# The first expert layer of blocks 6 to 17 as a one-level Strassen step

## The chip, the cores and the metric

The kernel runs on one core of one Trainium2 chip. The core has a matrix engine (TensorE: PE for matmuls, PEld for loading their stationary operand), a vector engine (VectorE, DVE), a scalar engine (ScalarE, ACT), a general engine (GpSimd, POOL) and 16 DMA engines, whose transfers are all issued here from SyncE (SP). Each engine takes its instructions strictly in order, and waits at the head of its queue on semaphores of the others. Matmuls write to PSUM, of which the kernel uses 8 banks of 512 f32 words in each of 128 partitions; everything else lives in SBUF. The metric is the device time of one execution in microseconds (us).

## The reference

Attention over keys and values that are first averaged in groups of eight, then a two-layer expert with a rational function between the layers:

```python
k_p = k.reshape(B, H, Sp, pool, D).mean(axis=3)        # 8 x 8 heads, 576 -> 72 keys
v_p = v.reshape(B, H, Sp, pool, D).mean(axis=3)
attn = softmax(q @ k_p.T / sqrt(D))                    # with 1e-9 added to the sum
x = (attn @ v_p), heads side by side                   # 4608 tokens x 512
h = x @ w_in                                           # 512 -> 2048
P = a[0] + a[1] * h + a[2] * h*h + a[3] * h*h*h
Q = 1.0 + abs(b[0]) * abs(h) + abs(b[1]) * h*h
out = (P / (Q + 1e-06)) @ w_out                        # 2048 -> 512
```

## The kernel before

The 4608 tokens are 18 blocks of 256 (index i), the 2048 columns of d_ff are 8 units of 256 (index u). For each (i, u):

- `mm1` (L783) makes h in a PSUM tile `ph`, two groups of 128 columns by 256 tokens. Every f32 factor is split into a high and a low part, and three products are added (high x high, low x high, high x low). The width of 512 is four slices of 128, so this is 2 x 3 x 4 = 24 matmuls with 256 columns.
- `rational` and `quotient` (L796, L812) compute P / Q on 512 words per partition: six ACT operations, five of DVE and two of POOL, with the tiles `t`, `w`, `r` in SBUF and the bank `rp` in PSUM. They end with `gh` and `gl`, the high and low part of the result.
- `mm2` (L833) multiplies these by `wout` into two banks `po`, which collect over the 8 units: 12 matmuls with 512 columns.

Attention for a block (`attend`, L733) runs ahead of its eight units: scores `ps`, exponentials `e`, transposes (by DMA pieces into `am` from block 4 on, from `e` in 32 x 32 squares), values `pv`; `values` splits the block's x into two tiles by an ACT copy and a DVE subtraction. `load_weights` (L456) rebuilds each of the 16 weight tiles (`win0` to `win7`, `wout0` to `wout7`) from its loaded words, and they stay in SBUF. Blocks 0 and 1 go through units 0 to 3 first, their x is stored to HBM, and units 4 to 7 follow later with x loaded back (`xr`): the reloaded halves.

Nothing is issued as it is written. `Plan` collects the operations with their tile dependences, due times (`due`, L889) and costs, `solve` (L166) is a list scheduler on those numbers, and `issue` (L252) writes the resulting order out for each engine. Where that order leaves PE a gap, `issue` puts matmuls whose moving operand is zero: into the tile `idle` in the start, later into an open `po` bank, one after the other until the planned gap is full. They are called fillers here. The planner's numbers set the order alone; how long anything takes on the chip is up to the chip. PSUM's 8 banks are handed out by the same planner, and so are the numbered buffers of each pool.

Every instruction passes through one line of `issue`, L284 (fillers: L276), so the profile's rows are told apart by the names of tiles.

## Time and profile before

| | before |
|---|---|
| median of 3 runs | 944.45 us (944.35 to 945.45) |
| profiled execution, from first to last instruction | 943.9 us |
| granted TensorE clock | 1.000 |
| instructions of DVE, ACT, POOL | 1336, 1124, 463 |
| DMA: bytes moved, mean rate | 75.33 MB, 80 GB/s |

The page gives each engine's busy time as a share of the span, groups of equal instructions with their count, total and mean, and ahead of each group how long its engine was idle and what ended that. PE's end times are modelled, since matmuls are pipelined; start to start is the safer reading. Idle time of an engine that nobody waits for costs nothing. A transfer is given by its packets and by the time from issue to landing.

### The profile page before, as it was taken

The numbers are of one execution on the slowest core, as the hardware profiler recorded it, in microseconds if no ns is written. First come the engines' busy times: TensorE is split into PE (matmuls) and PEld (weight loads), VectorE is DVE, ScalarE is ACT, GpSimd is POOL, SyncE is SP. The second block draws the span as 40 slices with busy tenths as digits, with TensorE's granted clock in tenths as the row PEclk, the third lists the DMA queues.
The fourth block names the chain that finished last, engine by engine and source line by source line (L and its number), as shares of the span: only waits on it lengthen the run. The fifth ranks groups of instructions, "written<-read, shape, count | busy, mean of one in ns | idle before, by whom it ended". The sixth has DMA issues, their size and how long they took to land.

```text
span 943.9 us, 17079 instructions
## 1 busy us (share of the span) xinstructions
PE 932.3 (99%) x6152; PEld 845.0 (90%) x6152; DVE 786.0 (83%) x1336; ACT 693.7 (73%) x1124; POOL 528.0 (56%) x463
## 2 busy tenths in 40 slices
PE   8899999999999999999999999999999999999998
PEld 8888998989988899998999899998999899999996
DVE  7799988788989888887887997888898987887664
ACT  4788889868675877686776777676868595868674
POOL 4776866866446544445634574447545663544443
PEclk9999999999999999999999999999999999999999
DMA  9994201254235322122603160316222421202000
GB/s 275 313 390 160 45 29 46 67 127 87 49 81 105 86 34 47 29 56 53 138 5 75 51 140 8 54 37 139 47 36 50 97 50 28 51 1 57 1 23 23
DMA packets 185365, 75.33 MB, mean 80 GB/s; under 512 B 162624, under 2 KB 162624, under 8 KB 185280
## 3 DMA queue, kind: packets, MB, share of 16 engines
q1 hardware_dynamic: 185280, 74.23, 31.2%
q8 instruction: 49, 0.80, 0.4%
q14 instruction: 36, 0.29, 0.1%
HBM read 50.60 MB, written 12.58 MB: 67 GB/s over the span
## 4 chain that ended last, share of the span: by engine, by line
PE 87%; DMA 3%; SPq 3%; DVE 3%; POOL 1%; ACT 1%; issue 1%; POOLq 0%; ACTq 0%
PE ph L284 39%; PE po L284 39%; PE pv L284 4%; PE ps L284 4%; SPq L284 3%; DMA q<-in_q_dram 1%; DMA early<-in_v_dram 1%; DVE sm L284 1%; DMA st_v<-in_v_dram 1%; DVE t L284 1%; POOL w L284 0%; PE pvs L284 0%; ACT rp L284 0%; PE pq L284 0%; DVE mx L284 0%
## 5 line engine op out<-in xcount | busy, mean ns | idle before, releaser
L284 PEld LDWEIGHTS ph<-x,win 128*128 128x128 f32 x3264 | 472.7, 188 | 55.5 <-ACT w L284 0.8
L284 PE MATMUL ph<-x,win 128*128 128x256 f32 x3264 | 495.7, 282 | 1.4 <-DVE x L284 0.5
L284 PE MATMUL po<-wout,gh 128*128 128x512 f32 x1152 | 353.1, 397 | 0.1
L284 POOL TENSOR_TENSOR w<-w,r 128x512 f32<-128x512 f32 (+1 forms) x145 | 191.1, 1318 | 230.3 <-ACT r L284 228.1
L284 POOL TENSOR_TENSOR gl<-t,gh 128x512 fp32r<-128x512 f32 (+1 forms) x145 | 193.3, 1333 | 93.1 <-ACT gh L284 91.9
L284 PEld LDWEIGHTS po<-wout,gh 128*128 128x128 f32 x1152 | 185.7, 189 | 12.5 <-POOL wout L284 0.8
L284 PE MATMUL po<-wout,gl 128*128 128x512 f32 x576 | 181.8, 396 | 0.3 <-POOL gl L284 0.3
L284 ACT ACTIVATE rp<-w,cbias 128x512 f32<-128x512 f32 (+1 forms) x145 | 99.6, 687 | 59.8 <-POOL w L284 56.6
L284 DVE SCALAR_TENSOR_TENSOR t<-t,abn,rp 128x512 f32<-128x512 f32 (+1 forms) x145 | 107.3, 740 | 38.4 <-ACT rp L284 35.3
L284 DVE TENSOR_TENSOR t<-t,ph 128x512 f32<-128x512 f32 (+1 forms) x145 | 97.8, 675 | 48.7 <-ACT t L284 46.7
L284 ACT ACTIVATE r<-w,abn 128x512 f32<-128x512 f32 (+1 forms) x145 | 117.9, 813 | 20.8 <-POOL gl L284 11.4
L284 ACT ACTIVATE t<-ph,abn 128x512 f32<-128x512 f32 (+1 forms) x145 | 111.0, 767 | 26.3 <-PE ph L284 23.0
L284 ACT ACTIVATE w<-ph 128x512 f32<-128x512 f32 (+1 forms) x145 | 85.7, 591 | 40.8 <-PE ph L284 34.4
L284 DVE SCALAR_TENSOR_TENSOR t<-t,abn,ph 128x512 f32<-128x512 f32 (+1 forms) x145 | 107.0, 738 | 5.2 <-ACT w L284 1.3
L284 ACT CAST gh<-t 128x512 fp32r<-128x512 f32 (+1 forms) x145 | 88.3, 609 | 20.5 <-DVE t L284 16.9
L284 DVE SCALAR_TENSOR_TENSOR t<-rp,t 128x512 f32<-128x512 f32 (+1 forms) x145 | 99.4, 685 | 4.1
L284 DVE SCALAR_TENSOR_TENSOR rp<-w,rp 128x512 f32<-128x512 f32 (+1 forms) x145 | 99.0, 683 | 0.2
L284 PEld LDWEIGHTS po<-wout,gl 128*128 128x128 f32 x576 | 93.0, 189 | 6.4 <-POOL gl L284 0.5
L284 ACT ACTIVATE rp<-rp 128x512 f32<-128x512 f32 (+1 forms) x145 | 84.1, 580 | 3.6 <-DVE t L284 0.5
L284 POOL TENSOR_TENSOR e<-e,sm 128x576 f32<-128x576 f32 x36 | 41.8, 1175 | 51.2 <-DVE sm L284 38.7
L284 POOL TENSOR_TENSOR st_v<-st_v 128x512 f32<-128x512 f32 (+1 forms) x36 | 36.3, 1015 | 17.4 <-DMA st_v<-in_v_dram 10.7
L284 PE MATMUL ps<-kpT,qT 128*128 128x144 f32 (+1 forms) x320 | 45.6, 292 | 0.4 <-DVE kpT L284 0.2
(101 smaller groups left out, 855.9 us busy)
## 6 DMA issues: line engine op xcount, KB each, us to landing
am<-e SPq DMA_DIRECT2D x224, 48.0 KB, 2.1
out_dram<-ob SPq DMA_DIRECT2D x17, 512.0 KB, 3.1
rwin<-in_moe_w_in_dram SPq DMA_DIRECT2D x8, 1024.0 KB, 11.1
rwout<-in_moe_w_out_dram SPq DMA_DIRECT2D x8, 1024.0 KB, 14.1
st_k<-in_k_dram SPq DMA_DIRECT2D x12, 512.0 KB, 4.8
st_v<-in_v_dram SPq DMA_DIRECT2D x12, 512.0 KB, 4.2
q<-in_q_dram SPq DMA_DIRECT2D x144, 32.0 KB, 2.0
st_v<-in_v_dram SPq DMA_DIRECT2D x48, 64.0 KB, 2.2
```

The costliest lines, as they stand in the source:

```text
L284: getattr(engines[op.eng], name)(*map(value, args), **{k: value(v) for k, v in kw.items()})
```

## The change

For blocks 6 to 17, two neighbouring blocks go through the units together (a pair; with a unit, a pair-unit). Their h is a product of two 2 x 2 block matrices: two groups of 128 columns of d_ff by two halves of the width, times two halves of the width by two blocks. Instead of eight block products a one-level Strassen step (Winograd's form) makes seven, each of 2 slices x 3 split products = 6 matmuls with 256 columns. In order of issue they are called product 1 to 7 below:

- `combine` makes the seven combinations of x for a pair, four subtractions on POOL and seven splits into high and low part (ACT copy, POOL subtraction), once for the pair. `values` now only copies x out of PSUM.
- `combine_w` makes the seven combinations of each `win` tile once, in the stretch of blocks 4 and 5 and the reloaded halves, and stores them to HBM (`wd`). `fetch` loads them again for every pair-unit, in two loads of 1 MB and 0.75 MB into three buffers in turn; the room of `win0` to `win7` serves for this, for the combinations of x and for a second `e`.
- `mm1_both` runs the seven products in two banks, one of which is both blocks' `ph` tile by halves. Product 1 goes to the first half of bank A and product 2 to the second. ACT then copies the first half of A to the first half of B, and the second half of A to `ys` in SBUF. Product 3 adds into B, product 4 into the first half of A. DVE then writes B plus `ys` over the second half of A, product 5 adds to that, product 6 adds into B, DVE writes B plus `ys` into B's second half, and product 7 adds to B's first half.
- From block 6 on the quotient works in `ph` itself, with no bank for `rp`. The `po` banks of both blocks of a pair, four, are open at once.
- Blocks 4 and 5 go ahead of the reloaded halves. The planner's costs are other numbers, its random shifts of due times are gone, and two pools differ in size. Behind the transposes of k, two matmuls by zero now follow (`pk`, `pl`).

```diff
-    LAT = 0.07
-
-    BEGIN = {"sp": 0.8, "pe": 1.7, "pool": 1.3, "dve": 1.5, "act": 1.5}
+
+
+    TAIL = {"sp": 0.0, "pe": 0.16, "pool": 0.06, "dve": 0.09, "act": 0.1}
+    HOP = {"sp": 0.035, "pe": 0.035, "pool": 0.08, "dve": 0.035, "act": 0.035}
+
+    BEGIN = {"sp": 0.8, "pe": 2.1, "pool": 1.3, "dve": 1.5, "act": 1.5}
     WARM = 8.6
 
     LOOK = 0.02
 
-
-    MOVED, SHARE, REACH = 1850, 0.03, 4.0
-    SHIFTS = (600170, 650652, 293686, 721265, 222299, 972752, 932340, 238443, 467684, 409349, 642869, 707107)
+    RATE = 410e3
...
-                    self.nc.tensor.matmul(to, lhsT=self.filler, rhs=one, start=first, stop=first)
+                    self.nc.tensor.matmul(to, lhsT=self.filler, rhs=one, start=first, stop=first,
+                                          skip_group_check=True)
...
+    pool("ys", 1)
+    PLAIN, AHEAD, TURNS = 6, 7, 4
+    SOON, CWD = {4: 25, 5: 20, 6: 40, 7: 0}, 40
...
+    dve = Engine(plan, "dve", 0.068, 1.04)
+    act = Engine(plan, "act", 0.06, 0.85)
+    gp = Engine(plan, "pool", 0.14, 2.15)
...
+        if n > 1:
+            for x in (pk, pl):
+                pe(118, [mm(x[:, 0:TOK], identr, zero.to_broadcast([P, TOK]), True, True)])
...
+            if two:
+                act(2 * TOK).copy(whole[:, 2 * c + i % 2], pv.rearrange("p j t -> p (j t)"))
+                continue
...
+    OVER = lambda i, u: i >= PLAIN
...
+    def combine(k):
+
+        x = raw_x[k]
+        t = new("dec", "m", [P, 2, 2 * TOK], F32, f"tt{k}")
+        x11, x12, x21, x22 = (x[:, n] for n in range(4))
+        t3, t2 = t[:, 0], t[:, 1]
+
+        def minus(out, a, b):
+            gp(2 * TOK).tensor_tensor(out=out, in0=a, in1=b, op=ALU.subtract)
+
+        def put(n, src):
+            pair, half = divmod(n, 2)
+            if not half:
+                at = len(PAIRS) % 5
+                PAIRS.append(new("cpool", ("win0", "win1", "win2", "x0", "x1")[at],
+                                 [P, 2, 2, 2, TOK], F32R, f"x{k}_{pair}"))
+            to = PAIRS[-1]
+            src = src.rearrange("p (c t) -> p c t", c=2)
+            act(2 * TOK).copy(to[:, half, 0], src)
+            gp(2 * TOK).tensor_tensor(out=to[:, half, 1], in0=src,
+                                      in1=to[:, half, 0].bitcast(F32), op=ALU.subtract)
+            return to[:, half]
+
+        minus(t3, x22, x12)
+        minus(x12, x12, x11)
+        minus(t2, x22, x12)
+        out = [put(0, x11), put(1, t3), put(2, t2), put(3, x21)]
+        minus(x21, x21, t2)
+        return out + [put(4, x21), put(5, x12), put(6, x22)]
...
+    def combine_w(u):
...
+        for out, a, b, op in ((s3, a11, a21, ALU.subtract), (s1, a21, a22, ALU.add),
+                              (s2, s1, a11, ALU.subtract), (s4, a12, s2, ALU.subtract)):
+            (gp if op is ALU.add or out is s4 else dve)(2 * P, port=True).tensor_tensor(
+                out=out, in0=a, in1=b, op=op)
...
+        for t in range(2):
+            for n, c, f in ((0, 0, 0), (3, 2, 0), (4, 2, 1)):
+                dma(128, o[:, n, t], v[:, t, c:c + 2, f, :], run=512)
+        for h in halves:
+            act(CW // 2).copy(hi[:, h], s[:, h])
+            gp(CW // 2).tensor_tensor(out=lo[:, h].bitcast(F32R), in0=s[:, h],
+                                      in1=hi[:, h].bitcast(F32), op=ALU.subtract)
+        for t, part in enumerate((hi, lo)):
+            part = part.bitcast(F32).rearrange("p (n x) -> p n x", n=4)
+            for n in range(2):
+                dma(256, d[:, 1 + 4 * n:3 + 4 * n, t], part[:, 2 * n:2 * n + 2], run=1024)
...
+    def fetch(u):
+        out = []
+        for n0, n1 in ((0, 4), (4, 7)):
+            at = len(fetched) % 3
+            fetched.append(at)
+            w = new("cpool", f"win{4 + at}", [P, n1 - n0, 2, 2, P], F32R, f"ww{u}_{n0}")
+            kb = (n1 - n0) * 256
+            dma(kb, w.bitcast(F32).rearrange("p n t c x -> p (n t c x)"),
+                sums[u][:, n0:n1].rearrange("p n t x -> p (n t x)"), run=8192, early=20.0)
+            out += [w[:, n] for n in range(n1 - n0)]
+        return out
+
+    def mm1_both(i, u, xs):
+
+        ws = fetch(u)
+        pa, pb = (bank(f"ph{i + m}_{u}", [P, 2, TOK]) for m in range(2))
+        ys = new("ys", "ys", [P, TOK], F32, f"ys{i}_{u}")
+        if u == 0:
+            for m in range(2):
+                pos[i + m] = [bank(f"po{i + m}_{u}_{n}", [P, DM]) for n in range(2)]
+        flying[i, u] = turn(f"turn{i}_{u}")
+
+        def product(n, out, first, last, after=()):
+            w, x = ws[n], xs[n]
+            terms = [(c, *wx) for wx in ((0, 0), (1, 0), (0, 1)) for c in range(2)]
+            return pe(118.1 * 6, [
+                ("matmul", (out,), dict(lhsT=w[:, wi, c, :], rhs=x[:, xi, c, :],
+                                        start=first and n_ == 0, stop=last and n_ == 5,
+                                        skip_group_check=True))
+                for n_, (c, wi, xi) in enumerate(terms)], claims=(pa, ys, flying[i, u]), after=after)
+
+        a, x, b, y = pa[:, 0], pa[:, 1], pb[:, 0], pb[:, 1]
+        p1 = product(0, a, True, False)
+        p7 = product(1, x, False, False, after=(p1,))
+        c1 = act(TOK, after=(p1, p7)).copy(b, a)
+        c2 = act(TOK).copy(ys, x)
+        p6 = product(2, b, False, False)
+        p2 = product(3, a, False, True, after=(c2,))
+        o2 = dve(TOK, after=(p2,)).tensor_tensor(out=x, in0=b, in1=ys, op=ALU.add)
+        product(4, x, False, True)
+        p5 = product(5, b, False, False, after=(o2,))
+        o3 = dve(TOK).tensor_tensor(out=y, in0=b, in1=ys, op=ALU.add)
+        product(6, b, False, True, after=(o3,))
+        return pa, pb
...
-        rp = bank(f"rp{i}_{u}", [P, 2, TOK])
+        rp = ph if OVER(i, u) else bank(f"rp{i}_{u}", [P, 2, TOK])
...
+    order += [(i, u) for i in range(4, PLAIN) for u in range(NU)]
     order += [(i, u) for i in range(2) for u in range(NA, NU)]
-    order += [(i, u) for i in range(4, NBLK) for u in range(NU)]
-    HEAD, PACE, SLOW, SLOWS = 15.0, 5.9, 5.0, 2 * NA
+    order += [(i, u) for i in range(PLAIN, NBLK, 2) for u in range(NU)]
+    HEAD, PACE, SLOW, SLOWS = 15.0, 5.6, 5.0, 2 * NA
+    ONE, TWO = 8 * NA + (PLAIN - 4) * NU, 10.8
...
+        if i >= PLAIN:
+            if i not in xs:
+                plan.slack = 1.4
+                for m in range(2):
+                    plan.now = due(at - AHEAD + 3 * m) - SOON.get(i + m, 0)
+                    attend(i + m)
+                plan.now = due(at)
+                xs[i] = combine(i // 2)
+            ph = mm1_both(i, u, xs[i])
+            for m in range(2):
+                plan.now = due(at + 2) + m * 1.5
+                gh, gl = rational(i + m, u, ph[m])
+                mm2(i + m, u, gh, gl)
+            continue
+        if (i, again) not in xs and i in SOON:
+            plan.slack = 1.4
+            plan.now = due(at) - SOON[i]
+            xs[i, again] = attend(i)
+            plan.now = due(at)
+        if i == 4 and u == 0:
+            for uu in range(NU):
+                plan.now = due(at - 8 + 3 * uu) + CWD
+                combine_w(uu)```

What the planner makes of it is seen in the order. In the rows, `ph10_3` is h of block 10, unit 3; `po10_0_0` an output bank of block 10; the last number of a name only counts instances; x4 is four in a row.

PE, block 10, unit 3, before: `ph` and `po` matmuls alternate, and none of them works on what another engine just made of `ph`.

```order
L284 MATMUL ph10_3_6780<-x0_10_6473,win3_850 128x256 x4
L284 MATMUL po9_0_0_6190<-wout7_2237,gh9_7_6605 128x512
L284 MATMUL po9_0_1_6192<-wout7_2237,gh9_7_6605 128x512
...
L284 MATMUL ph10_3_6780<-x1_10_6477,win3_850 128x256 x4
L284 MATMUL po9_0_0_6190<-wout7_2237,gl9_7_6633 128x512
L284 MATMUL po9_0_1_6192<-wout7_2237,gl9_7_6633 128x512
```

PE, blocks 10 and 11, unit 3, now, with `x5_0` to `x5_3` the combinations of x and `ww3` the fetched weights. Where "..." stands first, the two `po10` rows ahead of it come once more.

```order
L292 MATMUL ph10_3_7525<-x5_0_6120,ww3_0_7386 128x256 x12
L292 MATMUL po10_0_0_7404<-wout1_942,gh10_1_7498 128x512
L292 MATMUL po10_0_1_7406<-wout1_942,gh10_1_7498 128x512
...
L292 MATMUL ph11_3_7551<-x5_1_6947,ww3_0_7386 128x256 x6
L292 MATMUL ph10_3_7525<-x5_1_6947,ww3_0_7386 128x256 x6
L292 MATMUL po11_0_0_7439<-wout1_942,gh11_1_7545 128x512
L292 MATMUL po11_0_1_7441<-wout1_942,gh11_1_7545 128x512
...
L292 MATMUL ph11_3_7551<-x5_2_6976,ww3_4_7448 128x256 x6
...
L292 MATMUL ph10_3_7525<-x5_2_6976,ww3_4_7448 128x256 x6
L292 MATMUL ph11_3_7551<-x5_3_7014,ww3_4_7448 128x256 x6
```

Products 1 and 2 are the first row, 3 and 4 the next two of `ph`, then 6, 5 and 7. Between product 2 and product 3 stand four `po` matmuls, between 4 and 6 six.

ACT at the same place, before: the quotients of two units, one operation after the other.

```order
L284 ACTIVATE rp10_2_6840<-rp10_2_6840 128x512
L284 ACTIVATE w10_3_6856<-ph10_3_6780 128x512
L284 ACTIVATE r10_3_6865<-w10_3_6856,abn_325 128x512
L284 ACTIVATE t10_3_6875<-ph10_3_6780,abn_325 128x512
L284 ACTIVATE vm01_863<-vs5_6687,masks_124 128x4x64
```

ACT now, around the two copies of the pair-unit (`ph11_3` from `ph10_3`, and `ys10_3`).

```order
L292 ACTIVATE r10_2_7523<-w10_2_7507,abn_319 128x512
L292 ACTIVATE t11_2_7534<-ph11_2_7413,abn_319 128x512
L292 CAST gh11_1_7545<-t11_1_7427 128x512
L292 COPY ph11_3_7551<-ph10_3_7525 128x256
L292 COPY ys10_3_7556<-ph10_3_7525 128x256
L292 ACTIVATE w11_2_7568<-ph11_2_7413 128x512
```

The copies stand among the quotients of unit 2, behind a cast that reads what DVE made for unit 1.

PE where block 6 begins, before: its first matmuls lie among the `po` of block 5, and no filler is near.

```order
L284 MATMUL ph5_7_4051<-x1_5_3526,win7_1856 128x256 x4
L284 MATMUL ph6_0_4160<-x0_6_4127,win0_386 128x256 x8
L284 MATMUL ps14_0_4175<-kpT1_205,qT14_3772 128x144 x2
L284 MATMUL ps14_1_4178<-kpT1_205,qT14_3772 128x144 x2
L284 MATMUL po5_0_0_3846<-wout4_1973,gh5_4_4076 128x512
```

PE now, where the first pair-unit begins, after the reloaded units of block 1; L283 are fillers.

```order
L292 MATMUL ph6_0_4452<-x3_0_3622,ww0_0_4219 128x256 x6
L283 MATMUL po1_4_1_4488<-zero_87,identr_86 128x256 x12
L292 MATMUL ph6_0_4452<-x3_1_3674,ww0_0_4219 128x256 x6
L283 MATMUL po1_4_1_4488<-zero_87,identr_86 128x256 x3
L292 MATMUL ph7_0_4647<-x3_1_3674,ww0_0_4219 128x256 x6
L283 MATMUL po1_4_1_4488<-zero_87,identr_86 128x256 x5
L292 MATMUL ph7_0_4647<-x3_2_4617,ww0_4_4374 128x256 x6
L283 MATMUL po1_4_1_4488<-zero_87,identr_86 128x256 x3
```

Twenty-three fillers stand in this piece, and 25 more among the rows ahead of it. On po there are 121 in the whole order, before 10; in the tile `idle` 45, before 66.

More of the change, by code (lines that the diff above doesn't have):

```diff
@@ L368, in mm @@
     def mm(out, lhsT, rhs, start, stop):
-        return "matmul", (out,), dict(lhsT=lhsT, rhs=rhs, start=start, stop=stop)
+        return "matmul", (out,), dict(lhsT=lhsT, rhs=rhs, start=start, stop=stop,
+                                      skip_group_check=True)
     def dma(kbytes, dst, src, run=2048, issue=0.48, early=60.0, after=()):
@@ L707, in values @@
     def values(i, hi, lo):
-        xs = [new("work2", f"x{s}", [P, NJ, TOK], F32R, f"x{s}_{i}") for s in range(2)]
+        two = i >= PLAIN
+        if two:
+            xs = whole = both_x(i // 2)
+        else:
+            whole = new("cpool", f"x{i % 2}", [P, 2, NJ, TOK], F32R, f"x_{i}")
+            xs = [whole[:, s] for s in range(2)]
         for c in range(2):
@@ L777, in reload @@
     def reload(i, kept):
-        xs = [new("work2", f"x{s}", [P, NJ, TOK], F32R, f"xr{s}_{i}") for s in range(2)]
+        whole = new("cpool", f"x{i % 2}", [P, 2, NJ, TOK], F32R, f"xr_{i}")
+        xs = [whole[:, s] for s in range(2)]
         for x, d in zip(xs, kept):
```

139 lines of the change are left out of this document (90 added, 49 removed).

## The prediction

> **What bounds the kernel now.** The first view is the page: its span, the busy shares and the chain that ended last. Nearly every instruction passes through one helper line (L284), so the names of tiles, not lines, tell the stages apart.
>
> ```profile
> span 943.9 us, 17079 instructions
> PE 932.3 (99%) x6152; PEld 845.0 (90%) x6152; DVE 786.0 (83%) x1336; ACT 693.7 (73%) x1124; POOL 528.0 (56%) x463
> PE 87%; DMA 3%; SPq 3%; DVE 3%; POOL 1%; ACT 1%; issue 1%; POOLq 0%; ACTq 0%
> ```
>
> PE is busy 99% of the span and is 87% of the chain. The second view, busy time by stretch (PE, PEld, DVE, ACT, POOL, then clock, DMA share, GB/s), says where it isn't full.
>
> ```profile
> 0.00:50.00 50.00, 44.21 (x320) 41.06 (x321) 37.40 (x76) 30.49 (x58) 32.56 (x68) 1.00 0.97 298
> 50.00:100.00 50.00, 49.44 (x339) 43.72 (x339) 44.69 (x71) 43.46 (x69) 35.91 (x21) 1.00 0.66 239
> 100.00:150.00 50.00, 50.00 (x329) 45.56 (x329) 45.75 (x70) 42.66 (x69) 36.17 (x28) 1.00 0.14 36
> 900.00:944.00 44.00, 39.49 (x229) 33.87 (x227) 24.19 (x39) 26.10 (x45) 16.94 (x15) 1.00 0.07 25
> sum 300.00, PE 300.00 PEld 273.36 DVE 254.25 ACT 217.40 POOL 155.84; mean PE 50.00 PEld 45.56 DVE 42.38 ACT 36.23 POOL 25.97
> ```
>
> The last row sums 550 to 850 us: PE without a gap, clock 1.00, DVE at 84.8%, ACT at 72.5%, POOL at 51.9%. So in the blocks that change, a matmul taken away is its own length, unless another engine ends last in its place. The third view, PE's rows in order of time (start, us), prices a matmul by start to start, since one (282 ns in its group, the last row) overlaps the next.
>
> ```profile
> 499.85 0.64 PE L284 MATMUL ph<-x,win 128*128 128x256 f32 x4
> 500.32 0.64 PE L284 MATMUL po<-wout,gh 128*128 128x512 f32 x2
> 500.80 0.63 PE L284 MATMUL ph<-x,win 128*128 128x256 f32 x4
> 501.27 0.62 PE L284 MATMUL po<-wout,gl 128*128 128x512 f32 x2
> 501.73 0.63 PE L284 MATMUL ph<-x,win 128*128 128x256 f32 x4
> ...
> L284 PE MATMUL ph<-x,win 128*128 128x256 f32 x3264 | 495.7, 282 | 1.4 <-DVE x L284 0.5 <-ACT w L284 0.4 <-ACT t L284 0.3
> ```
>
> Four of 256 columns take 0.47 us, two of 512 take 0.465: 0.1175 and 0.2325 us each.
>
> The Trainium skill (TensorE: Matmul & The Clock Gate, Back-to-back issue gap) gives a lone warm matmul its columns over 2.4 plus 2.5 ns, 109 ns here. By it the products below would save 31.4 us instead of 33.8; the rows show 117.5, and they decide.
>
> **The change, part by part.** The sum is made on the profiled execution, 943.9 us; the median of the runs, 944.45, lies 0.55 above and is added at the end.
>
> *Products.* For two blocks and one unit of d_ff, 48 matmuls of 256 columns become 7 products of 6, 42. Over 48 pair-units that is 288 less: 288 x 0.1175 = **33.8 us off PE**. The order bears it out (3,456 ph matmuls, then 3,168; po stays at 1,728), so "it doesn't do what it says" is not among my rivals.
>
> *Fillers.* The program puts matmuls with zeros where its order has nothing for PE to run. They are instructions and cost PE time whether or not a wait occurs. On po there are 121, before 10: 111 x 0.1175 = **13.0 us added**. 48 of them stand at the switch to the first pair, 39 in the start, 10 at the end. Fillers of the start's idle tile go from 66 to 45; the last 22 of before are this row:
>
> ```profile
> 21.02 2.87 PE L276 MATMUL idle<-identr 128*128 128x256 f32 x22
> 23.73 0.39 PE L284 MATMUL idle<-identr 128*128 128x128 f32 x2
> ```
>
> 22 in 2.71 us, so 21 fewer are 2.6 us. Twelve new matmuls that follow the transposes of k (6 in pk, 6 in pl) add 1.4. **PE's balance: -33.8 + 13.0 - 2.6 + 1.4 = -22.0 us.**
>
> *Work for the other engines.* The nearest rows for the new operations:
>
> ```profile
> L284 ACT CAST am<-pr 128x256 fp32r<-128x256 f32 x8 | 2.8, 379 | 1.4 <-PE pr L284 1.4
> L284 DVE TENSOR_TENSOR am<-pr,am 64x256 fp32r<-64x256 f32 x8 | 3.2, 426 | 1.3 <-ACT am L284 1.2
> L284 DVE TENSOR_TENSOR x<-pv,x 128x512 fp32r<-128x512 f32 x36 | 24.5, 687 | 8.0 <-ACT x L284 8.0
> L284 ACT CAST x<-pv 128x512 fp32r<-128x512 f32 x36 | 20.9, 585 | 6.0 <-PE pv L284 5.4
> L284 POOL TENSOR_TENSOR gl<-t,gh 128x512 fp32r<-128x512 f32 x143 | 191.8, 1341 | 90.1 <-ACT gh L284 88.9 <-PE ps L284 0.9
> L284 DVE TENSOR_TENSOR st_k<-st_k 128x512 f32<-128x512 f32 x10 | 8.4, 854 | 0.0
> L284 DVE TENSOR_SCALAR ob<-po x12: 685/692/692, 310.3 to 857.0; 128x512 f32<-128x512 f32 x12
> ```
>
> The last row is one output eviction per block: 546.7 us in 11 steps, 49.7 a block, 99.4 for two. A pair loses 48 x 0.1175 = 5.6 of PE and lasts 93.8. DVE had 84.8% of 99.4 = 84.3; it gains 16 adds of 0.426 and loses 4 subtractions of 0.687: 88.3, or **94%**. ACT had 72.0 and gains 16 copies of 0.379 and 7 casts of 0.585: 82.2, 88%. POOL had 51.6 and gains 11 operations of 1.341: 66.4, 71%. None passes PE, so I cost this at nothing; without that cover it is DVE that comes next (a rival). The sums of the weights, made once in blocks 4 and 5 and the reloaded halves, are 16 DVE operations of up to 0.854 and 16 of half the size, some 20 us, with 33 on POOL. They lie in 24 units, at 49.7 / 8 some 150 us, of which DVE at 84.8% leaves 23 free; between nothing and 20 I take nothing.
>
> *New waits.* Within a pair-unit PE depends twice on another engine: product 3 needs an ACT copy made after product 2, and products 5 and 6 need a DVE add made after product 4. In the order of unit 3 of blocks 10 and 11, four 512-column matmuls (0.93 us) stand between product 2 and product 3. The last matmul's tail (0.282 - 0.1175), the copy (0.379) and a hand-over of 0.03 (the chain row of PE's end at 922.20 and ACT's start) take 0.57, leaving 0.36. On ACT the copies stand behind a cast of gh, which itself waits for DVE. The rows are of the chain, of ACT in order of time, and of the waits (total, times, longest):
>
> ```profile
> 921.72 0.48 PE ph L284 x4
> 922.23 0.61 ACT w L284
> ...
> 502.05 0.82 ACT L284 ACTIVATE r<-w,abn 128x512 f32<-128x512 f32 x1 [0.92 <-POOL gl L284]
> 502.77 0.60 ACT L284 CAST gh<-t 128x512 fp32r<-128x512 f32 x1
> ...
> ACT rp L284 <- POOL w L284: 56.6, 63, 3.1
> ```
>
> An ACT instruction is up to 0.72 from start to start; if one comes late in front of the copy, PE stands 0.36 us, with all of mm2 queued behind it. Bounds: nothing in any unit, and 48 x 0.36 = 17.3 in all. ACT was held up by POOL's w in 63 of 145 quotients, 43%, the nearest row for how often ACT runs late: **+7.5 us**. The DVE add has six 512-column matmuls, 1.40 us, to hide 0.62; one more DVE operation (0.69) fits, so nothing.
>
> *Weights fetched again.* Each pair-unit loads 7 x 256 KB through three buffers, 88 MB in all, issued from SP.
>
> ```profile
> q1 hardware_dynamic: 185280, 74.23, 31.2%
> rwout<-in_moe_w_out_dram SPq DMA_DIRECT2D x8, 1024.0 KB, 14.1
> xr<-xd SPq DMA_DIRECT2D x4, 512.0 KB, 3.6
> am<-e SPq DMA_DIRECT2D x224, 48.0 KB, 2.1
> ```
>
> A 1 MB load lands between 3.6 us (half the size on a quiet queue) and 14.1 (all weights at once). From the product that frees a buffer to the one that needs its next content the order has some 11.4 us of PE work. I take a load near the quiet row, hidden.
>
> **Sum:** 943.9 - 22.0 + 7.5 + 0.55 = **930.0 us**.
>
> **The rivals.**
>
> *DVE becomes the bound.* For: 94% in the pairs, above the 91.5% (45.75 of 50) that is its fullest stretch before. Against: that stretch had no need of more, and DVE instructions overlap where one doesn't need the other:
>
> ```profile
> 500.51 0.75 DVE L284 SCALAR_TENSOR_TENSOR t<-t,abn,rp 128x512 f32<-128x512 f32 x1
> 501.17 0.69 DVE L284 SCALAR_TENSOR_TENSOR rp<-w,rp 128x512 f32<-128x512 f32 x1
> 501.90 0.69 DVE L284 SCALAR_TENSOR_TENSOR t<-rp,t 128x512 f32<-128x512 f32 x1
> ```
>
> The second starts 0.66 us after the first, which takes 0.75; the third needs the second, and starts 0.73 after it. Were 91.5% its most, a pair would last 88.3 / 0.915 = 96.5, 2.7 over, 16.2 for six pairs: 943.9 - 22.0 + 16.2 + 0.55 = **938.7 us**. It eats the whole gain only below 90.6%.
>
> *The fetch lands late, slower.* Place: the weight buffers, in the stretch of each block where SP also issues the small pieces of am and q. Price: at 14.1 us against 11.4, PE waits 2.7 a time; once in each of the 12 blocks is 32.4, and 943.9 - 22.0 + 32.4 + 0.55 = **954.9 us**. It decides from 11.4 us on. For: SP is in order, and a waiting load holds those behind it. Against: 14.1 was taken with the queues 97% busy. At the first stretch's 298 GB/s and 0.97, 88 MB are 287 us of full queues, 0.51 of the six pairs' 563 us, beside the 0.31 of before.
>
> The Trainium skill (DMA: Bandwidth & Descriptors, Anatomy of one DMA) fits 2.0 us plus bytes over 436 GB/s, 4.4 us for 1 MB. By it this rival is out; it gives 3.2 for the 512 KB reload, where the row shows 3.6.
>
> *Everything is hidden, and the start is fuller.* Before, PE stood 5.79 and 0.56 us in the first two stretches, 2.1 of it ahead of its first matmul:
>
> ```profile
> PE idle L284 <- DVE identr L930: 2.1, 1, 2.1
> ```
>
> If the start's 39 fillers stand in place of the other 4.3 and no copy is late: 943.9 - 22.0 - 4.3 + 0.55 = **918.2 us**.
>
> **How the numbers follow.** Forecast 0.60 (own range 922 to 937), DVE bound 0.18, fetch late 0.10, all hidden 0.12. The range runs from 917 to 943: it takes in the lowest case, the forecast and most of the DVE case, and leaves out the late fetch and a little at each end. A difference under 0.2%, 1.9 us, can't be told from no change. Faster by more is the forecast, the hidden case and most of the DVE case, 0.60 + 0.12 + 0.15 = 0.87; within it the rest of the DVE case, 0.03; slower the late fetch, 0.10.
>
> **What would show it.** Product count: 288 fewer ph matmuls, at 0.1175 start to start. The copies: PE's idle time ahead of ph, released by ACT's copies, near 7 us in all; near zero, or above 17, says the term is mis-sized. DVE bound: PE waiting for DVE or ACT in every pair with DVE over 90%. Fetch: PE waiting for DMA at ph. The switch: no real work runs in the fillers' place. If the pairs last more than 97 us each, the step "none passes PE" is wrong.

## The result, and the profile after

The changed kernel takes **976.87 us** (median of four runs, 975.8 to 980.15) against 944.4 for the kernel before on the same chip (943.39 to 945.45): a ratio of 1.0347 [1.0327, 1.0367]. It is slower; the forecast was 930.0 with a range of 917 to 943.

The page of after: span, busy time, and the chain by engine and by line. After's one line of `issue` is L292 (in the experiments it lies some lines further down).

```profile
span 978.1 us, 17580 instructions
PE 930.6 (95%) x5966; PEld 822.1 (84%) x5966; DVE 790.5 (81%) x1440; ACT 738.8 (76%) x1278; POOL 637.9 (65%) x561
PE 38%; DMA 18%; DVE 13%; ACT 12%; SPq 10%; POOL 4%; issue 4%; DVEq 0%; ACTq 0%; POOLq 0%
```

PE's idle time grew from 11.6 us (943.9 - 932.3) to 47.5, and PE's share of the chain fell from 87% to 38%. DMA, the vector engines and SP's sequencer now end last in turn. No other engine has become the one that is full: DVE's share went down, from 83% to 81%. The idle time isn't all that PE lost: by the rows of before its matmuls are 22 us less, and its busy time fell by 1.7 only (932.3 to 930.6). Three stretches of 3.41 us at half clock explain 5.1 of this; the rest lies between matmuls that the page counts as busy, since their ends are modelled.

Where the idle time lies, by stretch. First before's start, then rows of after:

```profile
0.00:350.00 350.00, 342.99 (x2300) 310.94 (x2301) 301.33 (x510) 266.79 (x434) 224.67 (x213) 1.00 0.45 127
```

```profile
0.00:350.00 350.00, 333.58 (x2213) 298.83 (x2214) 297.06 (x535) 260.85 (x436) 245.87 (x237) 1.00 0.58 167
550.00:850.00 300.00, 285.25 (x1800) 249.16 (x1800) 241.57 (x451) 230.54 (x406) 190.93 (x158) 0.99 0.71 193
900.00:950.00 50.00, 50.00 (x316) 44.83 (x315) 37.06 (x60) 39.15 (x67) 24.25 (x19) 1.00 0.53 174
```

9.4 us more are lost in the first 350 us, before any pair runs. From 550 to 850, where PE had no gap, it now stands 14.75 of 300. From 900 on, in the last pair, beside which no attention for later blocks is prepared, PE is full again, although each pair-unit still has its copies, its DVE add and its fetches. So none of these stops PE by itself in these 50 us; they lose where attention is prepared beside them.

The first products of the first and of the last pair (start, duration):

```profile
356.52 0.87 PE L292 MATMUL ph<-x,ww 128*128 128x256 f32 x6
...
874.31 1.11 PE L292 MATMUL ph<-x,ww 128*128 128x256 f32 x8
```

Five pairs in 517.8 us are 103.6 each (the first shares its start with the last units of block 1); the forecast had 93.8 for a pair's PE work, and named 97 as the length from which "none passes PE" is wrong.

The DMA queue and its issues (KB each, median us from issue to landing):

```profile
q1 hardware_dynamic: 220864, 177.00, 63.4%
ww<-wd SPq DMA_DIRECT2D x48, 1024.0 KB, 5.8
ww<-wd SPq DMA_DIRECT2D x48, 768.0 KB, 4.9
am<-e SPq DMA_DIRECT2D x224, 48.0 KB, 4.0
```

The small pieces of the attention, `am`, took 2.1 us before and take 4.0 now. One place shows how this reaches PE. SP's instructions, then PE's, in order of time (in brackets how long PE stood, and for what):

```profile
469.90 0.44 SPq L292 DMA_DIRECT2D q<-in_q_dram  x1
470.74 0.34 SPq L292 DMA_DIRECT2D ww<-wd  x1
471.13 2.58 SPq L292 DMA_DIRECT2D am<-e  x4
473.81 1.04 SPq L292 DMA_DIRECT2D ww<-wd  x2
474.90 1.85 SPq L292 DMA_DIRECT2D am<-e  x2
```

```profile
472.01 0.63 PE L292 MATMUL po<-wout,gl 128*128 128x512 f32 x2
472.48 0.49 PE L283 MATMUL po<-zero,identr 128*128 128x256 f32 x3
476.26 0.94 PE L292 MATMUL ph<-x,ww 128*128 128x256 f32 x6 [3.28 <-DMA ww<-wd]
```

The fetch stands behind a row of pieces of `am` and `q`, most of them 0.44 to 0.66 us of SP, is issued at 470.74 and lands 5.38 us later; PE stands 3.28. The last product that read its buffer had ended at 458.39, so the buffer had been free for 12.35 us. The four pieces behind it land after it, from 476.30 to 476.85. On SP an issue can also wait for an earlier transfer; such waits for a fetch come to 39.6 us in the view of SP's waits:

```profile
SPq L292 <- DMA ww<-wd: 39.6, 35, 3.4
```

### The profile page after: what moved, and what is told of

It reads as the page before. It is cut to its first block, busy times and chain, and to the rows that moved or that the text cites. A ratio compares the mean times of both kernels' runs of the same rounds, so it can differ in the third digit from the quotient of the medians.

```text
span 978.1 us, 17580 instructions
## 1 busy us (share of the span) xinstructions
PE 930.6 (95%) x5966; PEld 822.1 (84%) x5966; DVE 790.5 (81%) x1440; ACT 738.8 (76%) x1278; POOL 637.9 (65%) x561
## 3 DMA queue, kind: packets, MB, share of 16 engines
q1 hardware_dynamic: 220864, 177.00, 63.4%
## 4 chain that ended last, share of the span: by engine, by line
PE 38%; DMA 18%; DVE 13%; ACT 12%; SPq 10%; POOL 4%; issue 4%; DVEq 0%; ACTq 0%; POOLq 0%
PE ph L292 17%; PE po L292 16%; SPq L292 10%; DMA ww<-wd 9%; DVE t L292 5%; DMA am<-e 4%; DMA q<-in_q_dram 3%; PE pv L292 3%; PE ps L292 2%; ACT w L292 2%; ACT t L292 2%; ACT r L292 2%; ACT gh L292 1%; ACT ph L292 1%; POOL gl L292 1%
## 5 line engine op out<-in xcount | busy, mean ns | idle before, releaser
L292 PE MATMUL po<-wout,gh 128*128 128x512 f32 x1152 | 341.7, 398 | 2.6 <-ACT gh L292 1.7
L292 PEld LDWEIGHTS ph<-x,ww 128*128 128x128 f32 x2016 | 263.0, 190 | 43.8 <-ACT ph L292 13.2
L292 PE MATMUL ph<-x,ww 128*128 128x256 f32 x2016 | 276.4, 284 | 17.9 <-ACT ph L292 8.5
L292 POOL TENSOR_TENSOR gl<-t,gh 128x512 fp32r<-128x512 f32 (+1 forms) x145 | 191.9, 1325 | 132.2 <-ACT gh L292 126.1
L292 POOL TENSOR_TENSOR w<-w,r 128x512 f32<-128x512 f32 (+1 forms) x145 | 189.5, 1307 | 87.9 <-ACT r L292 82.1
L292 PEld LDWEIGHTS po<-wout,gh 128*128 128x128 f32 x1152 | 194.8, 188 | 29.5 <-ACT gh L292 4.5
L292 DVE SCALAR_TENSOR_TENSOR t<-t,abn,ph 128x512 f32<-128x512 f32 (+1 forms) x242 | 178.2, 738 | 48.5 <-ACT ph L292 30.0
L292 PE MATMUL po<-wout,gl 128*128 128x512 f32 x576 | 182.4, 398 | 2.8 <-POOL gl L292 2.6
L292 PEld LDWEIGHTS ph<-x,win 128*128 128x128 f32 x960 | 134.1, 189 | 14.1 <-DVE t L292 1.1
L292 DVE TENSOR_TENSOR t<-t,ph 128x512 f32<-128x512 f32 (+1 forms) x145 | 98.1, 678 | 58.8 <-ACT t L292 50.4
L292 PE MATMUL ph<-x,win 128*128 128x256 f32 x960 | 141.3, 282 | 0.5 <-DVE t L292 0.3
L292 ACT CAST gh<-t 128x512 fp32r<-128x512 f32 (+1 forms) x145 | 89.4, 616 | 57.7 <-DVE t L292 53.6
L292 ACT ACTIVATE r<-w,abn 128x512 f32<-128x512 f32 (+1 forms) x145 | 118.1, 815 | 3.0 <-POOL gl L292 1.4
L292 PEld LDWEIGHTS po<-wout,gl 128*128 128x128 f32 x576 | 101.4, 189 | 22.2 <-POOL gl L292 5.3
L292 ACT ACTIVATE t<-ph,abn 128x512 f32<-128x512 f32 (+1 forms) x145 | 112.2, 775 | 8.9 <-PE ph L292 7.5
L292 ACT ACTIVATE w<-ph 128x512 f32<-128x512 f32 (+1 forms) x145 | 86.2, 595 | 38.5 <-PE ph L292 25.8
L292 ACT ACTIVATE ph<-w,cbias 128x512 f32<-128x512 f32 (+1 forms) x97 | 66.7, 688 | 23.0 <-POOL w L292 19.8
L292 POOL TENSOR_TENSOR e<-e,sm 128x576 f32<-128x576 f32 x36 | 42.2, 1188 | 38.9 <-DVE sm L292 29.8
L292 DVE SCALAR_TENSOR_TENSOR t<-ph,t 128x512 f32<-128x512 f32 (+1 forms) x97 | 66.0, 681 | 1.8 <-ACT ph L292 0.5
L292 DVE SCALAR_TENSOR_TENSOR ph<-w,ph 128x512 f32<-128x512 f32 (+1 forms) x97 | 66.0, 682 | 0.1
L292 ACT ACTIVATE ph<-ph 128x512 f32<-128x512 f32 (+1 forms) x97 | 56.4, 581 | 2.1 <-DVE ph L292 0.4
L292 DVE TENSOR_TENSOR ph<-ph,ys 128x256 f32<-128x256 f32 x96 | 40.9, 426 | 18.0 <-PE ph L292 13.7
## 6 DMA issues: line engine op xcount, KB each, us to landing
ww<-wd SPq DMA_DIRECT2D x48, 1024.0 KB, 5.8
ww<-wd SPq DMA_DIRECT2D x48, 768.0 KB, 4.9
rwin<-in_moe_w_in_dram SPq DMA_DIRECT2D x8, 1024.0 KB, 10.7
rwout<-in_moe_w_out_dram SPq DMA_DIRECT2D x8, 1024.0 KB, 9.7
```

The costliest lines, as they stand in the source:

```text
L292: getattr(engines[op.eng], name)(*map(value, args), **{k: value(v) for k, v in kw.items()})
```

## The experiments

C, Q, D and N stand for the copies, the fetches in SP's queue, the vector engines and the planner's numbers. All are edits of after unless said otherwise, and times are medians. The kernel before took 943.4 to 944.0 us beside them. `no_copy_wait`, `no_refetch`, `small_refetch`, `both_off`, `light_dve`, `light_quotient` and `light_dve_fetch` leave out a part of the computation; the others make the whole of it.

### The copies inside a pair-unit

`no_copy_wait`: both ACT copies and the first DVE add work on a zero and on `ys` in SBUF, so neither PE nor they wait for each other there; product 3 then begins its bank afresh.

```diff
+        c1.swap = [("copy", (d1, d0), {})]
+        c2.swap = [("copy", (ys, d0), {})]
...
+        o2.swap = [("tensor_tensor", (), dict(out=d2, in0=d0, in1=ys, op=ALU.add))]
```

> The changed kernel with every engine's order as it is, but both ACT copies and the first DVE add of each pair-unit work on constants in SBUF with the same 256 columns, so that PE waits for none of the three (h of these blocks is wrong; the second add is kept). Theory C expects 20 us or more less than 976.9, under 957. Theory Q expects only the direct hand-overs, which the trace puts at under 15 us, to go, and PE to stand later instead: over 965. Theory N: over 965.

982.49 us, ratio 1.0404 [1.0387, 1.0421]: no gain at all, but 5.6 us more than after, with a granted clock of 0.989 to 0.991 against 0.994 to 0.995. The waits were there. After's list of waits (us, times, longest) has

```profile
PEld ph L292 <- ACT ph L292: 13.2, 14, 2.5
PE ph L292 <- ACT ph L292: 8.5, 10, 2.0
PE ph L292 <- DMA ww<-wd: 5.9, 3, 3.3
```

but without them PE stands as long for something else, in no_copy_wait for instance

```profile
PE pv L294 <- DVE t L294: 6.4, 5, 2.1
PE po L294 <- ACT gh L294: 3.4, 8, 0.9
```

where after has 1.4 and 1.7. C falls as the cause.

### The fetches

`no_refetch` makes only the first load of each of the two kinds of fetch, and all products use that; `small_refetch` makes every fetch at its place, after the same waits, but from the second into each of the three buffers on with 16 KB instead of 1 MB or 768 KB. `fetch_by_act` and `fetch_by_pool` issue the whole fetches from another engine; `dma_rate_300` lets the planner count on slower transfers.

```diff
+            if op.once is not None:     # no_refetch
+                b = op.calls[0][1][0].tile
+                if op.once in loaded:
+                    b.it = loaded[op.once]
+                    continue
+                loaded[op.once] = b.real()
...
+            op.swap = [("dma_start", (w.bitcast(F32)[:, 2:4, 0, 1, 0:16],      # small_refetch
+                                      sums[0][:, 2:4, 0, 128:144]), {})]
...
+            plan.ops[-1].via = nc.scalar     # fetch_by_act; nc.gpsimd in fetch_by_pool
...
-    RATE = 410e3
+    RATE = 300e3     # dma_rate_300
```

> The changed kernel with every engine's order as it is, but 94 of the 96 weight loads of the pair-units left out (all units work with the weights of unit 0, so the output is not the reference's). Theory Q (queue): the 1 MB and 0.75 MB loads stand in SP's one transfer queue ahead of attention's small pieces, which then land late and hold SP, and the whole order slips; the trace has am<-e landing after 4.0 us in place of 2.1. It expects 25 to 40 us less than the 976.9 of the changed kernel, 937 to 952. Theory C (copies): PE stands for ACT's copies and DVE's adds inside the pair-units; it expects no change, over 970. Theory N (numbers): the planner's new cost numbers are too tight for the chip, so that the order slips everywhere; it expects no change from this edit either, over 970.

> Left out: after the first full load of each of the three fetch buffers, every fetch moves 16 KB in place of 1 MB or 768 KB (2 x 16 columns of 128 partitions), so the products use the first unit's weights. It stands at the same place in SP's queue and waits for the same buffer and semaphore. Theory B (the time that the bytes take, and the pieces that land behind them): as no_refetch, 956 to 962. Theory I (SP stands at the issue for the buffer to be free, and holds am and q behind it): 970 to 978.

> The whole computation. The 96 fetches are issued by ACT at the same place of the order, through its own queue; nothing else is changed. Theory Q (a fetch holds the small pieces behind it in the one queue, and the semaphores that are used in turn hold SP): the small pieces land in about 2 us again and the time falls toward no_refetch, 958 to 966. Rival B (what costs is the bytes, 88 MB on the same 16 DMA engines, whatever the queue): 973 to 980. Rival A (ACT stands at the issues for buffers that are not yet free): over 980.

> The whole computation. As fetch_by_act, but the 96 fetches are issued by POOL, which is busy least. Theory Q: 958 to 966, less where ACT lost time by its issues. Rival B (the bytes): 973 to 980. Rival A (POOL stands at the issues, or an issue takes it long): over 980.

> The changed kernel with one number of the planner changed: transfers are planned at 300 in place of 410 GB/s, near the 307 that the first stretch of before shows per full queue. The work is the same, the order is another. Theory Q expects the order to leave the loads their time: under 962. Theory N, where it is the transfers' number that is too tight, expects the same, and a gain in the stretch before 340 us too. Theory C expects 970 or more.

| | us | ratio to before |
|---|---|---|
| after | 976.87 | 1.0347 [1.0327, 1.0367] |
| no_refetch | 958.44 | 1.0150 [1.0134, 1.0166] |
| small_refetch | 959.15 | 1.0156 [1.0134, 1.0177] |
| fetch_by_act | 1000.76 | 1.0607 [1.0558, 1.0656] |
| fetch_by_pool | 1002.66 | 1.0610 [1.0581, 1.0640] |
| dma_rate_300 | 983.71 | 1.0420 [1.0404, 1.0435] |

The fetches cost 18 us: less than theory Q had (25 to 40), and not nothing, as C and N had. With the same issues at the same places but few bytes 17.7 of them come back, so it is what the bytes take that costs, not SP standing for a buffer. PE's own waits for a fetch in after are 5.9 us, 3 times (the row above); by which way the rest of the 18 reaches PE isn't shown. The issues of small_refetch:

```profile
am<-e SPq DMA_DIRECT2D x224, 48.0 KB, 2.1
```

and those of fetch_by_act, where the fetches go through ACT's queue and the pieces stay in SP's:

```profile
ww<-wd ACTq DMA_DIRECT2D x48, 1024.0 KB, 5.5
am<-e SPq DMA_DIRECT2D x224, 48.0 KB, 3.9
```

The pieces land as late as in after: theory Q, that it is the one queue that makes them late, falls, and its rival B, the bytes, stands for the landings. The Trainium skill (DMA: Bandwidth & Descriptors, Issuing engines are not separate DMA queues) says that DMAs of different engines end up on the same 16 DMA engines and interleave; the 3.9 us agree. The 24 and 26 us that these two kernels lose beyond after are in the range of rival A (over 980); in fetch_by_pool POOL stands 28.0 us, 16 times, for buffers in the middle of its own work (its waits between 350 and 860 us):

```profile
POOL ww L293 <- PE ph L293: 28.0, 16, 4.9
```

For ACT such stands are not shown. Planning for slower transfers makes more fillers (231 on `po` in place of 121) and no gain, but 6.8 us more than after.

### The vector engines

`both_off` joins no_refetch and no_copy_wait. `light_dve` is no_refetch with the five DVE operations of a quotient in the pairs on half their columns, `light_quotient` the same with most of ACT's and one of POOL's too, and `light_dve_fetch` is light_dve with the fetches.

```diff
+        half = lambda v: v[:, :, 0:P] if isinstance(v, Lazy) and v.tile in tiles else v
+        for op in plan.ops[at:] if done else ():
+            if op.eng in ("dve",):
+                op.swap = [(nm, tuple(map(half, ar)), {k: half(v) for k, v in kw.items()})
+                           for nm, ar, kw in op.calls]
```

> Left out: as in no_refetch, only the first load of each of the two kinds of fetched weights is made, and as in no_copy_wait, the two ACT copies and the first DVE add of each pair-unit read and write SBUF instead of the products' banks. The order on every engine is that of after. Theory Q+C (with the fetches there, PE waits for the queue of SP first and the waits for the copies lie inside those; with the queue free, it is the copies that end last, and they are what is left of the loss in the pairs: 19.3 us of PE and weight-load waits for ACT ph and DVE ph in no_refetch between 350 and 860 us): 958.4 - 19 = 939, so 935 to 945. Rival R (what is left has a third cause, the attention's own chain or the order): 953 to 960.

> Left out: as in no_refetch, all but the first load of each kind of fetched weights; and in the pairs, the five DVE operations of each quotient work on 256 of their 512 columns (480 operations, some 0.3 us shorter each, 144 us of DVE). The order on every engine is that of after. Theory D (with the queue free, what is left of the loss in the pairs is DVE and the chain of the quotient through it): 958.4 less at least 12 of the some 18 that the pairs lose there beyond no_pairs, so 938 to 947. Rival (neither; the waits are set by PE's own order or by the other engines): 953 to 960.

> As light_dve, and also four of the six ACT operations and one of the two POOL operations of each quotient in the pairs work on half their columns. Theory D: 936 to 945, hardly below light_dve. Theory A (it is ACT and POOL in the quotient's chain, not DVE): light_dve stays above 953 and this one falls to 940 to 948. Rival (none of the three): both 953 to 960.

> As light_dve (the five DVE operations of each quotient in the pairs on 256 of their 512 columns), but with all the fetches, as in after. Theory + (two losses that add up): 976.9 - 15 = 962, so 958 to 966. Theory H (the wait for the fetch hides DVE's, which ends last only once the queue is free): 972 to 978. Below 955 if a late DVE is what makes the fetches late.

| | us | ratio to before |
|---|---|---|
| both_off | 964.54 | 1.0208 [1.0186, 1.0230] |
| light_dve | 943.70 | 1.0004 [0.9989, 1.0020] |
| light_quotient | 937.94 | 0.9932 [0.9912, 0.9951] |
| light_dve_fetch | 969.73 | 1.0265 [1.0236, 1.0295] |

With the queue free, taking the copies away gains nothing either, against both expectations (935 to 945, 953 to 960); its four times run from 961.8 to 970.3, and the profile is that of the longest. PE and its loads then stand for the vector engines elsewhere, as both_off's waits between 350 and 880 us show (`pv` stood 1.3 us for DVE in no_refetch):

```profile
PE pv L301 <- DVE t L301: 5.8, 5, 2.2
PE ph L301 <- DVE ph L301: 3.0, 3, 1.6
PEld po L301 <- ACT gh L301: 3.2, 8, 1.0
```

Half the DVE work of the quotient is worth 14.7 us (958.4 to 943.7), and the lighter ACT and POOL another 5.8. Theory D holds. The loads of `ph` stood for DVE in no_refetch and hardly do in light_dve, and in no_refetch DVE itself stood for ACT, and ACT for POOL (350 to 860 us; the second row is light_dve's, the others are no_refetch's):

```profile
PEld ph L301 <- DVE ph L301: 7.1, 17, 1.7
PEld ph L301 <- DVE ph L301: 0.4, 2, 0.2
DVE t L301 <- ACT t L301: 21.3, 28, 2.4
DVE t L301 <- ACT ph L301: 20.3, 25, 1.9
ACT ph L301 <- POOL w L301: 16.8, 22, 1.4
```

The stretch of 550 to 850 us (PE, PEld, DVE, ACT, POOL) in no_refetch, light_dve and light_quotient:

```profile
550.00:850.00 300.00, 295.19 (x1874) 259.15 (x1873) 248.59 (x451) 241.92 (x428) 196.66 (x163) 1.00 0.23 50
```

```profile
550.00:850.00 300.00, 299.10 (x1922) 266.55 (x1921) 191.67 (x459) 246.28 (x438) 202.45 (x168) 1.00 0.22 49
```

```profile
550.00:850.00 300.00, 299.72 (x1943) 270.25 (x1942) 189.07 (x460) 209.16 (x444) 175.75 (x169) 1.00 0.22 49
```

PE's gap goes from 4.81 to 0.90 to 0.28. In no_refetch DVE is busy 82.9% while PE waits for it: it is late before it is full, and it waits for ACT, which waits for POOL, in the same chain. The lighter operations shorten both DVE's work and that chain; the two aren't told apart. With the fetches present the lighter DVE is worth only 7.1 us (976.9 to 969.7), between the two expectations, so the two losses partly hide one another.

### The planner

`no_pairs` is after with every block by itself, so without combinations, fetches and copies, but with its planner numbers and its order of blocks; `no_pairs_old_blocks` has before's order of blocks too, and asks for the attention of blocks 4 to 7 no sooner. `before_no_shifts` is the kernel before without its twelve shifts. `old_numbers` is after, pairs and all, with before's numbers, but not its shifts. `no_fillers` is after without the 121 fillers on `po`.

```diff
-    PLAIN, AHEAD, TURNS = 6, 7, 4
+    PLAIN, AHEAD, TURNS = 18, 7, 4     # no_pairs, no_pairs_old_blocks
...
-    SHIFTS = (600170, 650652, 293686, 721265, 222299, 972752, 932340, 238443, 467684, 409349, 642869, 707107)
+    SHIFTS = ()     # before_no_shifts
...
-    dve = Engine(plan, "dve", 0.068, 1.04)
+    dve = Engine(plan, "dve", 0.16, 1.04)     # old_numbers, likewise for the others
...
-                elif sums:
+                elif sums and False:     # no_fillers
```

> The changed planner, pools and block order, without the Strassen step: blocks 6 to 17 one at a time with 24 matmuls a unit, no sums of weights, no fetch. Theory N expects it slower than the kernel before by 10 us or more, over 954, as the first 340 us of the changed kernel lose some 12 us more of PE time than before without any fetch. Theories Q and C expect it within 5 us of before, under 950.

> The whole computation. As no_pairs (every block by itself, the planner's new numbers), and the blocks in the order of before, with the attention of blocks 4 to 7 asked for no sooner than there. It differs from before_no_shifts by the numbers, the pools and their use. Theory B (the order of the blocks): 946 to 952. Theory N (the numbers): 958 to 964.

> The whole computation: the kernel before, with the twelve hand-chosen shifts of due times left out, and nothing else changed. Theory S (what no_pairs lost against before is the order that those shifts had found, which the change drops): 955 to 965. Rival (the lost time of no_pairs lies in the new numbers or the order of the blocks): 944 to 949.

> The whole computation, pairs and fetches as in after; only the planner's numbers that set the order are those of before (one hand-over of 0.07 for all engines and no tails, the costs of PE, DVE, ACT and POOL, the start of PE, the rate of transfers). 72 fillers on po instead of 121. Theory N (the new numbers by themselves cost some 18 us, as no_pairs suggests): 955 to 962. Rival (what no_pairs lost comes from the dropped shifts of due times or from the order of the blocks, not from the numbers): 970 to 985.

> The kernel after without the 121 matmuls with zeros on po; all else, and the order, the same. The term of the forecast (a filler costs its length, 0.117 us, wherever it stands): 976.9 - 14 = 963. Rival W (PE would stand at those places anyway, so the time without them is spent waiting): 974 to 979. Rival G (the gaps make the clock fall by half more often): over 980.

| | us | ratio to before |
|---|---|---|
| no_pairs | 962.02 | 1.0197 [1.0176, 1.0219] |
| no_pairs_old_blocks | 957.30 | 1.0141 [1.0117, 1.0165] |
| before_no_shifts | 947.93 | 1.0038 [1.0026, 1.0051] |
| old_numbers | 1016.89 | 1.0767 [1.0734, 1.0800] |
| no_fillers | 978.45 | 1.0363 [1.0332, 1.0395] |

Without any pair the new plan is 18 us slower than before: 3.9 for the shifts, 9.4 between before_no_shifts and no_pairs_old_blocks, which differ by the numbers, the closers behind `pk` and `pl` and the pools, and 4.7 for the order of the blocks and the earlier attention. no_pairs has 74 fillers on `po`, before 10: at 0.1175 each the 64 more are 7.5 of the 18. Theory N of no_pairs holds, but it named the numbers alone. With the pairs the new numbers are better than the old ones, by 40 us, against my theory N and beyond its rival too (970 to 985). The expectation's 72 fillers were a count of rows; old_numbers has 504, and after 121:

```profile
L283 PE MATMUL po<-zero,identr 128*128 128x256 f32 x504 | 67.6, 277 | 0.0
```

```profile
L283 PE MATMUL po<-zero,identr 128*128 128x256 f32 x121 | 17.6, 275 | 0.0
```

383 more at 0.1175 are 45 us, near the difference of 40. That fits a filler that costs its length there, but the whole order differs too, and no run takes these fillers out. In after a filler doesn't cost its length: without the 121 the time is the same within its interval, since PE stands at those places instead.

### One pair

`last_pair_only` makes a pair of blocks 16 and 17 alone, with the sums of the weights made in blocks 14 and 15 and all else as in no_pairs_old_blocks; `last_pair_old` is the same with before's numbers.

```diff
-    PLAIN, AHEAD, TURNS = 6, 7, 4
-    SOON, CWD = {4: 25, 5: 20, 6: 40, 7: 0}, 40
+    PLAIN, AHEAD, TURNS = 16, 7, 4
+    SOON, CWD = {16: 40, 17: 0}, 40
...
-        if i == 4 and u == 0:
+        if i == 14 and u == 0:
```

> The whole computation. Only blocks 16 and 17 are a pair; all others run as in no_pairs_old_blocks, the sums of the weights are made in blocks 14 and 15. 48 products' matmuls less (5.6 us), 12 fillers on po more (1.4), 16 fetches. Theory P (a pair gains its matmuls where no attention lies beside it): 957.3 - 4.2 = 953, so 950 to 956. Rival (the sums of the weights, the fetches or the switch take it back): 957 to 964. In neither case below the kernel before.

> The whole computation. As last_pair_only, with the planner's numbers of before and no shifts; the nearest kernel is before_no_shifts, 947.9. 48 products' matmuls less (5.6 us), 60 fillers on po more (7.0). If a filler costs its length: 949 to 951. If the fillers stand where PE would wait anyway, as no_fillers showed of those in after: 942 to 946.

974.88 us, ratio 1.0321 [1.0304, 1.0339], and 988.39, 1.0468 [1.0453, 1.0484]: both far above either expectation. In last_pair_only most of it is one place, the switch to the pair:

```profile
800.00:850.00 50.00, 49.69 (x336) 45.12 (x335) 45.23 (x83) 37.44 (x62) 32.58 (x27) 1.00 0.35 94
850.00:900.00 50.00, 37.64 (x217) 32.45 (x216) 29.05 (x45) 30.38 (x54) 35.65 (x30) 0.90 0.61 186
900.00:950.00 50.00, 50.00 (x318) 44.95 (x317) 35.43 (x57) 39.36 (x68) 25.46 (x20) 1.00 0.48 160
```

12.4 us of PE idle time, and a clock of 0.90 in the mean. The longest stand, 6.1 us, is one of `ph` for ACT's part of the combinations of x. They need both blocks' attention, and where that comes is set by the kernel's `SOON`; that another place would do better was not tried. So whether a pair gains by itself stays open; last_pair_only measured mostly the switch, and last_pair_old, with 13.2 us of PE's idle time in the same 50 us, in part. No kernel of the study that computes everything beats the kernel before.

## Why the prediction was wrong, point by point

*Products, closers, counts of fillers.* Right as counts: `ph` has 3,168 matmuls, `po` 121 fillers, and by the rows of before PE has 22 us less work. What went wrong is in what PE waits for, and for 5.1 us in its clock.

*"None passes PE, so I cost this at nothing."* This step failed. It compared DVE's share, 94%, with PE's. After's DVE share from 550 to 850 us is 80.5%, and its fullest 50 us in the pairs, 400 to 450, have 91.7%; in no_refetch DVE was late at 82.9%, in the stretch where attention runs beside the quotients. Halving DVE's part of the quotient returned 14.7 us once the fetches were gone, 7.1 with them. My rival's mark (91.5% busy) was wrong; that its 16.2 us lie near 14.7 is luck, since light_dve takes away more than the change had added: it doesn't split what DVE costs into the new adds and the rest. Counted as above, the pairs take 99.8 us in no_refetch and 97.0 in light_dve, so the mark of 97 is passed without the fetches too.

*"I take a load near the quiet row, hidden."* This step failed: 18.4 us. My rival had 32.4, and put it at loads that land in 14.1 us. The loads themselves landed after 5.8 and 4.9 us in the median, the longest after 10.4, under the 11.4 of cover:

```profile
DMA to landing us min/median/max: 4.1/5.3/10.4
```

That row is over all 96 fetches. What I left out is their neighbours: `am` and `q` land later, SP's next issues come later, and a fetch is issued late behind them: the 11.4 counted on an issue as soon as the buffer is free, and the fetch shown above was issued 12.35 us after that. By the Trainium skill (DMA: Bandwidth & Descriptors, Anatomy of one DMA), whose fit I gave as 4.4 us and which states it for transfers issued from GpSimd, this rival was out. Here the 1 MB loads took 5.8 in the median from SP and 5.9 from POOL, and the fetches cost 18.4 us without loads as slow as 14.1.

*New waits, +7.5.* This step failed too. The mechanism was seen (8.5 us of PE's idle time ahead of `ph` behind ACT's copies), but as a term it was wrong: taking the copies' waits away returned nothing, with or without fetches.

*Fillers, +13.0.* As a cost it was wrong here, since the same time is lost without them. That it is right where PE doesn't wait is likely by old_numbers, not shown.

*What the sum left out.* The planner's new numbers, the dropped shifts and the new order of blocks had no term, only the fillers that come of them. no_pairs puts them at 18 us for single blocks, with 7.5 us of fillers among them. They explain only a part of the 9.4 us of PE's idle time that after loses in the first 350 us: no_pairs, with the same numbers and order of blocks, loses 3.5 there.

```profile
0.00:350.00 350.00, 339.51 (x2267) 305.80 (x2268) 275.96 (x487) 255.09 (x422) 215.34 (x208) 1.00 0.42 123
```

The other 5.9 come with what the pairs need there. The sums of the weights, costed at nothing, run there (DVE is busy 297.06 us in place of 275.96); what they cost was not tried apart.

*The account.* After is 46.9 us above the forecast. 18.4 for the fetches, up to 20.5 for the vector engines and up to 18.0 for the plan make 56.9, and the terms of 7.5 and 13.0 that returned nothing stand on the other side. The parts hide one another, and the 18.0 hold fillers that the 13.0 had counted, so they don't add up to the difference, and I don't claim that they do. Without fetches and with most of the quotient's work halved, light_quotient still takes 937.9, 8 us above the forecast.

## What to carry to other kernels

A matmul taken away is gained only if the engines that feed PE keep their order in time: where several in-order engines wait for each other in one chain, PE can wait for an engine that is 83% busy, so price added work by what waits behind it and not by its share. Bytes that are hidden for the buffer they fill are not hidden for the small transfers beside them; check what those do to the next issue. And when a change brings a new order or new scheduling numbers, give them a term of their own, with the kernel before under that order as the first experiment.

## What the hardware showed

A wait of PE of 3.3 us was followed by a stretch at half clock. The stretches around the wait shown above (PE busy first; granted clock, DMA share and GB/s last):

```profile
472.90:476.30 3.40, 0.12 (x2) 0.07 (x1) 2.17 (x4) 0.62 (x1) 1.10 (x1) 1.00 1.10 272
477.70:481.10 3.40, 3.40 (x20) 2.81 (x18) 1.03 (x3) 3.24 (x7) 1.46 (x2) 0.50 1.07 359
481.20:484.60 3.40, 3.40 (x17) 2.88 (x18) 3.33 (x7) 2.58 (x5) 2.31 (x2) 1.00 1.06 178
```

So this wait cost again after it had ended. A shorter one can too: in after, half clock from 685.9 us on follows two stands of 1.43 and 1.23 us, and in no_copy_wait 10.24 us of it follow one of 2.10. The stretches at half clock last 3.41 us or a multiple and lie on one grid. Counted by it over after and the seventeen experiments, from 15 to 930 us, each of the 36 pieces of 3.41 us in which PE was idle for 1.95 us or more was followed by half clock, and 12 of the 34 with 1.6 to 1.95. The Trainium skill (TensorE: Matmul & The Clock Gate, Part 1: The HAM clock gate) has the clock at half after an idle window of about 3.4 us; the length of the pieces agrees, but PE needn't be idle for the whole of one.

48 KB pieces that take 2.1 us in a quiet queue took 4.0 with the fetches in their own queue, 3.9 with them in ACT's and 4.2 in POOL's: what these transfers cost their neighbours hardly depended on the queue that they were issued from.
